# A decode-attention kernel: ScalarE issues the first quarter of the query weights ahead of its small rows, SP the other three quarters

## The chip, the cores and the metric

The kernel runs on one core of a Trainium2 chip. The metric is device time in microseconds (us) for one launch, shown as the median of several runs. The profile names the engines PE (TensorE, matmul), PEld (its weight loads), DVE (VectorE), ACT (ScalarE), POOL (GpSimd) and SP (SyncE, which here only issues transfers). SP's and ACT's queues for DMA instructions are shown as SPq and ACTq; the packets that come from them run under the names q1 (SP) and q10 (ACT) on the same 16 DMA engines.

## What is computed

One token is decoded. Its row `x` (448 values) is normalised. Part A is attention: queries from `xn @ wq` for 16 heads of 256, over a cache of 8 key-value heads with 65536 positions each, then a product with `wo`. Part B is a small gated network on the same row, scaled by a sigmoid of `xn @ w_r`. The output is one row of 448 values.

```
xn = _layernorm(x)
q  = (xn @ wq).reshape(B, Sq, Hq, Dh)            # 448 x 4096 weights
scores = einsum("bhqd,bhkd->bhqk", q, k) * Dh**-0.5
o  = einsum("bhqk,bhkd->bhqd", softmax(scores), v) @ wo
r  = xn @ w_r
y  = (silu(xn @ w_gate) * (xn @ w_up)) @ w_down * sigmoid(r)
out = x + o + xn + y
```

The K and V caches are 256 MiB each in bf16, and every byte of them is read once.

## The kernel before

The caches come in units: one head's keys or values in four units of 8 MiB (128 positions for each of 128 partitions). SBUF holds a ring of three slots of this size. Keys go to slots 0 and 1 in turn, values to slot 2. The first five K units come as two halves (K0 first half, K0 second half, and so on), each with a semaphore of its own, later ones whole. Since all four K units of a head are needed before its softmax, the order is: K0 to K3, V0, K4, K5, then one V and one K unit in turn.

SP issues all the large loads in one list, in that order, and waits in the list: K2's first half needs the first half of slot 0 to be read by PE (`FREEH`), its second half needs all of slot 0 read (`FREE`), K3's halves the same of slot 1; V0 needs the query projection done, whose weights lie in slot 2. Ahead of K0 the list has the query weights `wq` in two parts, one quarter and three quarters of every partition's row, both on one semaphore.

Before PE's main loop there is a chain that makes the queries. ACT issues two small rows, `x` and `w_r` (896 bytes each), on one semaphore (`w0`). DVE first clears some tiles and then waits for both rows. Then come: a cast of x to fp32 (L368), its mean (L370, L372), the subtraction (L375), the sum of squares (L377, L380), a square root on ACT (L405), the scaling and a cast back (L383 to L387), copies that order the row (L393); PE turns it to columns, DVE copies these (L412 to L414), PE multiplies with `wq` (it waits for both parts), DVE scales the result (L416), PE transposes it, DVE copies it to `qT_sb` (L419). POOL fills constants meanwhile and at last clears `kt_all` (L356).

PE then enters its loop over K units. For each set of positions it transposes keys into `ps_t`, DVE (L490) and ACT (L492) copy them to `kt_all`, PE multiplies them with the queries into `ps_q`, ACT copies the scores (L514), PE transposes these into `ps_s`. From unit 4 on, each K unit is joined by one V unit of the head before. PE's last transpose on a slot frees it for SP.

All PE instructions have one line in the profile (L428), and all DMA issues L949, as helpers record them.

Of the kernel before, what the change touches and what calls it, by code (L numbers as in the profile page):

```python
# [22 lines left out]
def bass_parallel_sum__gqa_block_cached__moe_arch_mod__decode_kernel(  # L23
# [54 lines left out]
    WQN, WGN, WDN, WON = RP * HqDh // 2, RP * F, FH * D, rep * NH * D  # L78
# [17 lines left out]
    wq_area = slots[2][:, 0:WQN]  # L96
# [99 lines left out]
    prog = {e: [] for e in engines}  # L196
    here = [("S", 0)]
# [13 lines left out]
    def W(e, *key):  # L211
        put(e, "w", key, None, None)
# [3 lines left out]
    def O(e, key, fn, sem=None, n=1):  # L216
        key = key if isinstance(key, tuple) else (key,)
        if not ghost[0]:
            weight[key] = n
        put(e, "o", key, fn, sem or e)  # L220
# [19 lines left out]
    semtot = {}  # L240
    fed = {}

    def item(key, parts, need=()):
        for n in need:
            W("sp", *n)
        for ap, src, sem in parts:
            semtot[sem] = semtot.get(sem, 0) + 16
            items[key] = (sem, semtot[sem])
            prog["sp"].append(("d", here[0], ("DMA", key, len(prog["sp"])), (ap, src), sem))
# [16 lines left out]
    def flat_src(src, n):  # L266
        return src.rearrange("a b -> (a b)").rearrange("(p n) -> p n", p=P)
# [21 lines left out]
        slot_item("v", t, 2, None, [("VFREE", t - 1)] if t else [("QT",), ("R",), ("CONST",)])  # L289

    WQ1 = WQN // 4
    item("wq", [(wq_area[:, a:b], flat_src(A_wq, WQN)[:, a:b], "wq") for a, b in ((0, WQ1), (WQ1, WQN))])
    for u in range(U):
        k_item(u)
    v_item(0)
# [102 lines left out]

    def act_setup():
        a = nc.scalar  # L400
        for k, (d, s) in enumerate([(x_row, A_x[0]), (wr_row, B_w_r.rearrange("(o n) -> o n", o=1))]):
            prog["act"].append(("d", here[0], ("w0", k), (d, s), "w0"))
        items["w0"] = ("w0", 32)
        W("act", "VPE")
        O("act", "SQRT", lambda it: a.activation(out=stat[0:1, 3:4], in_=stat[0:1, 2:3], func=ACTF.Sqrt), "evq")  # L405
        W("act", "R")
        O("act", "SIG", lambda it: a.activation(out=stat[0:1, 6:7], in_=stat[0:1, 5:6], func=ACTF.Sigmoid), "ev3")
        W("dve", "XNT")
        x = ps_m[0:P, C_XNT:C_XNT + 2 * NE].rearrange("p (t r) -> p r t", t=2)
        xv = xnT_sb.rearrange("p (r b t) -> p r b t", b=2, t=2)  # L410
        y, z = xv[:, :, 0, :], xv[:, 0:NE - 1, 1, :]
        O("dve", "xnt0", lambda it: nc.vector.tensor_copy(out=y, in_=x), "exp")  # L412
        O("dve", "xnt1", lambda it: nc.vector.tensor_copy(out=z[:, :, 0], in_=x[:, 1:NE, 1]))
        O("dve", "XNTSB", lambda it: nc.vector.tensor_copy(out=z[:, :, 1], in_=x[:, 0:NE - 1, 0]))  # L414
        W("dve", "QROW")
        O("dve", "QROWSB", lambda it: nc.vector.tensor_scalar(  # L416
            out=q_row[0:QROWS, :], in0=q_rows[0:QROWS, :], scalar1=inv_sqrt_dh, scalar2=None, op0=ALU.mult))
        W("dve", "QT")
        O("dve", "QTSB", lambda it: nc.vector.tensor_copy(  # L419
            out=qT_sb[:, :, :], in_=ps_m[0:P, C_Q:C_Q + NH * Hq].rearrange("p (q f) -> p f q", f=NH)), "pc", 2)  # L420
        W("act", "QTSB")
        W("act", "S2Z")
# [482 lines left out]
    pool_setup()  # L905
    dve_setup()
    act_setup()
    pe_setup()
    for u in range(NU):
# [275 lines left out]
```

## Time and profile before

| | |
|---|---|
| time, median of 3 runs | 1275.9 us (1275.61 to 1275.92) |
| the profiled execution | 1275.73 us, span 1274.4 us |
| PE busy | 960.9 us, 75% |
| DVE busy | 576.2 us, 45% |
| ACT busy | 436.4 us, 34% |
| POOL busy | 11.6 us, 1% |
| read from HBM | 549.03 MB, 431 GB/s over the span |

Span is from the first to the last recorded instruction of the profiled execution. In a timeline's line stand start, duration, engine, code line, operation and tiles; the brackets at its end give the idle time of the engine ahead of it and what ended that. A DMA issue's last number is the time from issue to landing. In a table of windows each engine has its busy time and count, and the last three columns are PE's granted clock, the busy share of the DMA engines, and GB/s.

### The profile page before, as it was taken

What the parts mean: (1) busy time and instruction counts of PE and PEld (TensorE: products, weight loads), DVE (VectorE), ACT (ScalarE), POOL (GpSimd) and SP (SyncE); (2) the same over time, 40 slices, a digit from 0 to 9 for tenths busy, and PEclk for the clock granted to TensorE, in tenths of its full rate; (3) what the DMA queues carried; (4) which work ended last, traced back from release to release, by engine and by line L of the source; (5) the groups of instructions that cost most, each with busy time, mean ns of one, the idle gap of its engine ahead of it and who ended that gap; (6) DMA issues with size and microseconds to landing.
All of it is one profiled execution on the core that took longest, in us unless ns stands there. A gap on an engine that the chain in (4) does not pass through costs nothing.

```text
span 1274.4 us, 23463 instructions
## 1 busy us (share of the span) xinstructions
PE 960.9 (75%) x9691; PEld 623.0 (49%) x9691; DVE 576.2 (45%) x1083; ACT 436.4 (34%) x656; POOL 11.6 (1%) x38
## 2 busy tenths in 40 slices
PE   3898977778777679777778776787777787777674
PEld 2676654445544455444455444554444554444321
DVE  5666544355344455343454444453444544444310
ACT  1555433244332434233333243343333333323300
POOL 3000000000000000000000000000000000000000
PEclk9999988799888899887898888898888988888875
DMA  9999999999999999999999999999999999999998
GB/s 408 428 435 436 440 428 430 432 432 442 436 428 430 434 432 442 434 430 428 436 432 444 430 430 428 436 432 444 430 430 430 434 438 438 430 430 430 430 431 369
DMA packets 12356, 549.18 MB, mean 431 GB/s; under 512 B 1335, under 2 KB 1722, under 8 KB 2874
## 3 DMA queue, kind: packets, MB, share of 16 engines
q1 hardware_dynamic: 12340, 549.03, 99.8%
q8 instruction: 7, 0.11, 0.0%
q14 instruction: 3, 0.02, 0.0%
q10 hardware_dynamic: 6, 0.00, 0.0%
HBM read 549.03 MB, written 0.00 MB: 431 GB/s over the span
## 4 chain that ended last, share of the span: by engine, by line
DMA 77%; PE 19%; ACT 2%; issue 1%; DVE 1%; SPq 0%; ACTq 0%; DVEq 0%
DMA ring<-in_A_v_cache_dram 68%; PE ps_o L428 13%; DMA ring<-in_A_k_cache_dram 4%; PE ps_t L428 3%; DMA ring<-in_A_wo_dram 2%; DMA kt_all<-in_A_wo_dram 2%; PE ps_q L428 2%; ACT kt_all L492 1%; PE ps_m L428 1%; SPq L949 0%; DVE kt_all L490 0%; PE ps_s L428 0%; ACT S_sb L573 0%; DVE kt_all L731 0%; DVE ring L854 0%
## 5 line engine op out<-in xcount | busy, mean ns | idle before, releaser
L428 PE MATMUL ps_t<-ident_f,ring 128*128 128x128 f32 x4096 | 584.5, 284 | 75.3 <-DMA ring<-in_A_k_cache_dram 48.2
L490 DVE COPY kt_all<-ps_t 128x1024 bf16<-128x1024 bf16 x768 | 486.8, 684 | 281.7 <-PE ps_q L428 277.5
L428 PEld LDWEIGHTS ps_t<-ident_f,ring 128*128 128x128 f32 x4096 | 449.1, 143 | 226.7 <-issue 138.2
L492 ACT ACTIVATE kt_all<-ps_t 128x1024 bf16<-128x1024 bf16 x256 | 261.9, 1023 | 497.1 <-PE ps_q L428 497.0
L428 PE MATMUL ps_o<-ring,p_sb 128*4 128x512 bf16 x2040 | 184.7, 526 | 202.9 <-DMA ring<-in_A_v_cache_dram 198.5
L428 PEld LDWEIGHTS ps_o<-ring,p_sb 128*4 128x4 bf16 x2040 | 54.2, 104 | 295.5 <-issue 271.3
L428 PE MATMUL ps_q<-kt_all,q_cur 128*2 128x512 bf16 x2056 | 163.8, 395 | 0.4 <-DVE kt_all L490 0.3
L514 ACT ACTIVATE s<-ps_q 98x512 bf16<-98x512 f32 x257 | 151.6, 590 | 1.3 <-PE ps_q L428 1.3
L596 DVE RECIPROCAL rs<-ps_m 128x4 f32<-128x4 f32 x29 | 5.3, 183 | 278.5 <-PE ps_m L428 278.5
L583 ACT ACTIVATE p_sb<-S_sb 128x128 bf16<-128x128 bf16 x64 | 18.9, 307 | 269.6 <-PE ps_o L428 267.0
L428 PEld LDWEIGHTS ps_s<-sel_bf,s 128*128 128x128 bf16 x1032 | 64.5, 98 | 5.3 <-ACT s L514 1.9
L428 PE MATMUL ps_s<-sel_bf,s 128*128 128x8 bf16 x1032 | 63.6, 167 | 1.3 <-ACT s L514 1.3
L639 DVE CAST ob_sb<-ps_o 100x512 bf16<-100x512 f32 x29 | 20.1, 692 | 91.4 <-PE ps_o L428 91.4
L428 PEld LDWEIGHTS ps_q<-kt_all,q_cur 128*2 128x2 bf16 x2056 | 26.5, 79 | 43.6 <-issue 43.6
L428 PEld LDWEIGHTS ps_m<-rowsum,ones_f 128*128 128x128 f32 x58 | 12.5, 269 | 23.9 <-issue 23.9
L492 ACT ACT_TABLE_LOAD x7 | 9.0, 1283 | 21.7 <-PE ps_q L428 21.7
L543 DVE TENSOR_REDUCE m1p<-S_sb (+1 forms) x33 | 13.9, 422 | 4.4
L428 PE MATMUL ps_m<-rowsum,ones_f 128*128 128x4 f32 x58 | 15.1, 330 | 0.0
L541 DVE CAST S_sb<-ps_s 128x256 f32 (+1 forms) x33 | 13.7, 414 | 1.9 <-PE ps_s L428 1.9
L573 ACT ACTIVATE S_sb<-S_sb,negmax 128x512 bf16<-128x512 bf16 x16 | 13.2, 852 | 3.2 <-DVE negmax L567 3.2
L428 PE MATMUL ps_m<-diag,ones_f 2*128 2x2 f32 x58 | 11.2, 260 | 3.7 <-DVE diag L558 0.8
L428 PEld LDWEIGHTS ps_m<-diag,ones_f 2*128 2x128 f32 x58 | 8.7, 187 | 10.5 <-DVE diag L558 10.5
(97 smaller groups left out, 136.4 us busy)
## 6 DMA issues: line engine op xcount, KB each, us to landing
ring<-in_A_k_cache_dram SPq DMA_DIRECT2D x10, 4096.0 KB, 28.3
ring<-in_A_v_cache_dram SPq DMA_DIRECT2D x1, 4096.0 KB, 20.6
ring<-in_A_wq_dram SPq DMA_DIRECT2D x1, 2688.0 KB, 11.2
ring<-in_A_wo_dram SPq DMA_DIRECT2D x1, 2688.0 KB, 28.7
ring<-in_A_v_cache_dram SPq DMA_DIRECT2D x1, 2048.0 KB, 24.8
ring<-in_B_w_gate_dram SPq DMA_DIRECT2D x1, 1568.0 KB, 16.4
ring<-in_B_w_up_dram SPq DMA_DIRECT2D x1, 1568.0 KB, 19.8
ring<-in_B_w_down_dram SPq DMA_DIRECT2D x1, 1568.0 KB
```

The source lines that it names most:

```text
L428: return pe.matmul(*a, **k)
L490: O(e, ("EV", s, m), lambda it: nc.vector.tensor_copy(out=kt[:, :], in_=tb[:, :]), f"ev{m}")
L492: O(e, ("EV", s, m), lambda it: nc.scalar.activation(out=kt[:, :], in_=tb[:, :], func=ACTF.Copy), f"ev{m}")
L514: O("act", ("EVQ", s), lambda it: nc.scalar.activation(out=s2[s % 2][0:QROWS, :], in_=ps_q[0:QROWS, :], func=ACTF.Copy), "evq")
L541: O("dve", ("SCOPY", u), lambda it: nc.vector.tensor_copy(out=S_sb[:, at(it, SBN), :], in_=ps_sn), "sc")
L543: O("dve", ("SMAX", u), lambda it: nc.vector.tensor_reduce(out=m1p[:, :, at(it, 1)], in_=S_sb[:, at(it, SBN), :].rearrange("p n i -> p i n ...
L573: O("act", ("EXP", h, i), lambda it, i=i: nc.scalar.activation(out=S_sb[:, :, i], in_=S_sb[:, :, i], func=ACTF.Exp, bias=negmax[:, i:i + 1 ...
L583: O("act", ("PC", t, c), lambda it: nc.scalar.activation(out=p_sb[:, c, :, :], in_=S_sb[:, n:n + CH, :], func=ACTF.Copy), "pc")
L596: O("dve", ("RS", t), lambda it: nc.vector.reciprocal(out=rs[:, :, :], in_=ps_m[0:P, C_TOT:C_TOT + NH * rep]))
L639: O("dve", ("OB", t), lambda it: nc.vector.tensor_copy(out=ob_sb[0:OROWS, :], in_=ps_o[0:OROWS, :]))
```

## The change

The first quarter of the query weights leaves SP's list and becomes the first DMA that ACT issues, ahead of `x` and `w_r`. SP's list now begins with the other three quarters. The semaphore of the weights counts both as before (16 from each).

```
     WQ1 = WQN // 4
-    item("wq", [(wq_area[:, a:b], flat_src(A_wq, WQN)[:, a:b], "wq") for a, b in ((0, WQ1), (WQ1, WQN))])
+    wq_parts = [(wq_area[:, a:b], flat_src(A_wq, WQN)[:, a:b]) for a, b in ((0, WQ1), (WQ1, WQN))]
+    semtot["wq"] = 16
+    item("wq", [(*wq_parts[1], "wq")])
     for u in range(U):
         k_item(u)
...
     def act_setup():
         a = nc.scalar
+        prog["act"].append(("d", here[0], ("wq", 0), wq_parts[0], "wq"))
         for k, (d, s) in enumerate([(x_row, A_x[0]), (wr_row, B_w_r.rearrange("(o n) -> o n", o=1))]):
             prog["act"].append(("d", here[0], ("w0", k), (d, s), "w0"))
         items["w0"] = ("w0", 32)
```

More of the change, by code (lines that the diff above doesn't have):

```diff
@@ L291, in bass_parallel_sum__gqa_block_cached__moe_arch_mod__decode_kernel @@
     WQ1 = WQN // 4
-    item("wq", [(wq_area[:, a:b], flat_src(A_wq, WQN)[:, a:b], "wq") for a, b in ((0, WQ1), (WQ1, WQN))])
+    wq_parts = [(wq_area[:, a:b], flat_src(A_wq, WQN)[:, a:b]) for a, b in ((0, WQ1), (WQ1, WQN))]
+    semtot["wq"] = 16
+    item("wq", [(*wq_parts[1], "wq")])
     for u in range(U):
@@ L400, in act_setup @@
         a = nc.scalar
+        prog["act"].append(("d", here[0], ("wq", 0), wq_parts[0], "wq"))
         for k, (d, s) in enumerate([(x_row, A_x[0]), (wr_row, B_w_r.rearrange("(o n) -> o n", o=1))]):
```

## The prediction

> **What bounds the kernel now.** The page first: the slices, the queues and the chain.
>
> ```profile
> span 1274.4 us, 23463 instructions
> ...
> q1 hardware_dynamic: 12340, 549.03, 99.8%
> HBM read 549.03 MB, written 0.00 MB: 431 GB/s over the span
> DMA 77%; PE 19%; ACT 2%; issue 1%; DVE 1%; SPq 0%; ACTq 0%; DVEq 0%
> ```
>
> SP's queue (q1) keeps the 16 DMA engines busy for 99.8% of the span. At 549.03 MB nothing that an engine computes shows in the time, unless it leaves the DMA engines without work, at the start, at the end, or because SP issues a transfer too late. The change touches the start, so I go to the first microseconds of the DMA view (slices of 0.2 us) and to the timelines of SP and ACT.
>
> ```profile
> GB/s 0 0 0 0 0 0 0 0 143 251 220 143 143 179 358 430 358 466 435 430 358 538 757 645 358 108 466 753 430 108 430 753 430 108 430 753 430 108 430 753
> ...
> 1.00:2.00 1.00, 0.00 (x0) 0.00 (x0) 0.48 (x1) 0.48 (x1) 0.84 (x8) 1.00 0.50 79
> 2.00:3.00 1.00, 0.00 (x0) 0.00 (x0) 0.84 (x3) 0.80 (x1) 1.00 (x9) 1.00 0.68 209
> 3.00:4.00 1.00, 0.00 (x0) 0.00 (x0) 0.85 (x3) 0.00 (x0) 1.00 (x8) 1.00 1.04 424
> ...
> 0.74 0.86 SPq L949 DMA_DIRECT2D ring<-in_A_wq_dram  x2
> ...
> 0.73 0.52 ACTq L949 DMA_DIRECT2D ring<-in_A_x_dram  x1
> 1.28 0.21 ACTq L949 DMA_DIRECT2D ring<-in_B_w_r_dram  x1
> 1.52 1.28 ACT L405 ACT_TABLE_LOAD   x1 [1.52 <-PEq L1170]
> 13.43 0.20 ACT L405 ACTIVATE stat<-stat 1x1 f32<-1x1 f32 x1 [10.62 <-DVE stat L380]
> ```
>
> The first bytes move at 1.6 to 1.8 us, 0.9 to 1.1 after SP's first issue (0.74), and full rate is there by 4. SP and ACT both begin at 0.73 to 0.74, so the first byte cannot come earlier. What a fuller start could give is the shortfall against 431 GB/s between 1.75 and 4: (0.25 x 431 + 431) - (79 + 209) in the first two stretches, some 0.25 MB, or 0.6 us.
>
> **The change, part by part.** *SP loses its first issue* (0.86 / 2 = 0.43 us); everything behind it is issued 0.43 earlier. Worth nothing: the queue is full from 4 us on. In the first two us two queues now feed the engines: between +0.3 and -0.6 us (the shortfall above as the bound of the gain, half of it as that of a loss from switching queues); I take 0, since the bytes and the first issue are as before.
>
> *ACT gains one issue*, ahead of its small rows: 0.43 by SP's row, 0.52 by ACT's own first. Its table load moves from 1.52 to about 2.0, and still ends 10 us ahead of its use at 13.43: nothing. The weights land in sum when they did; their use is covered below.
>
> *The small rows go behind the first quarter.* This is the part that can cost. ACT's queue (q10) shares the 16 engines with q1. Four narrow stretches of the DMA view show how x and w_r get through now; the lines are those of 2.02:2.14, 2.14:4.42, 4.42:4.48 and 4.48:5.0.
>
> ```profile
> DMA packets 6, 0.03 MB, mean 246 GB/s; under 512 B 1, under 2 KB 2, under 8 KB 6
> q10 hardware_dynamic: 2, 0.00, 5.3%
> ...
> q1 hardware_dynamic: 107, 0.77, 88.5%
> q14 instruction: 1, 0.01, 1.5%
> ...
> DMA packets 6, 0.04 MB, mean 612 GB/s; under 512 B 2, under 2 KB 3, under 8 KB 5
> q10 hardware_dynamic: 2, 0.00, 5.2%
> ...
> DMA packets 31, 0.32 MB, mean 607 GB/s; under 512 B 13, under 2 KB 13, under 8 KB 18
> ...
> ring<-in_A_wq_dram SPq DMA_DIRECT2D x1, 2688.0 KB, 11.2
> ring<-in_A_wq_dram SPq DMA_DIRECT2D x1, 896.0 KB, 5.2
> ring<-in_A_k_cache_dram SPq DMA_DIRECT2D x1, 4096.0 KB, 20.4
> ```
>
> x passes at 2.02 to 2.14. w_r, issued 0.55 later, passes only at 4.42 to 4.48, 2.3 us after x. One engine's share of the first quarter is 896 KB / 16 at 431/16 GB/s, 2.13 us: w_r waited for just that share, then went ahead of the second part (rows of 8 KB and more begin in the same stretch), though that part had been issued 0.1 us before it. So I read an engine's turn as one transfer's whole share (8 rows and a semaphore write), with the two queues taking turns: x, first part, w_r, second part. After the change ACT's queue holds first quarter, x, w_r in that order, and SP's the three quarters, the first half of K0, the second half. Turns: quarter (2.13 us), three quarters (6.39), x, half of K0 (4096 KB: 9.73), w_r. From 2.05 that is 2.05 + 18.25 = 20.3; w_r now lands 0.6 before DVE starts (4.45 against 5.04 below), so DVE would start at 20.9 where it starts at 5.04.
>
> The Trainium skill, "DMA: Bandwidth & Descriptors", section "Queues, rings and completion order", says that an engine goes round its queue rows by packets and drains a packet, about 9 to 17 descriptors, before it switches. A share of 8 rows and a semaphore write is nine, so the trace's turn fits it; if instead the packet were filled by count, x and w_r with their two writes would share one turn, w_r would pass before K0, and the sum would be that of the second rival.
>
> *What waits for w_r*: DVE's first cast, and the whole query chain behind it. DVE's timeline:
>
> ```profile
> 5.04 3.75 DVE L368 CAST ring<-ring 1x448 f32<-1x448 bf16 x1 [0.69 <-DMA ring<-in_B_w_r_dram]
> 9.65 2.91 DVE L375 TENSOR_SCALAR ring<-ring,stat 1x448 f32<-1x448 f32 x1
> 13.85 0.44 DVE L385 TENSOR_SCALAR ring<-ring,stat 1x448 f32<-1x448 f32 x1
> 14.32 0.38 DVE L387 CAST ring<-ring 1x448 bf16<-1x448 f32 x1
> 20.61 0.19 DVE L419 CAST qT_sb<-ps_m 128x32 bf16<-128x32 f32 x1 [0.42 <-PE ps_m L428]
> ...
> 8.81 3.51 POOL L356 MEMSET kt_all<- 128x4096 bf16 x1
> ...
> 23.15 0.45 PE L428 MATMUL ps_t<-ident_f,ring 128*128 128x128 f32 x1 [2.65 <-issue]
> ```
>
> The chain takes 20.80 - 5.04 = 15.8 us. Two of its steps run long beside POOL (3.75 and 2.91, where the same work takes 0.38 and 0.44 once POOL is done at 12.3). Late, they cost 3.37 and 2.47 less: 9.9 us. So the chain ends at 20.9 + 9.9 = 30.8 instead of 20.8, and PE, which needs 2.65 us of its own between that chain and its first K transpose, starts at 33.2: 10.0 later. The first quarter of the weights is no issue: both parts land by 1.19 + 11.2 = 12.4.
>
> *Does a late PE matter?* PE frees the ring slots that SP waits for. PE's pace from its start, what it waited for, SP's issues, and issue to landing of the four K halves that need a freed half slot (issued at 35.7, 49.5, 60.9 and 72.3):
>
> ```profile
> 23.12:34.74 11.62, 11.50 (x102) 8.19 (x103) 6.61 (x12) 4.62 (x7) 0.00 (x0) 0.86 1.00 430
> 34.74:72.31 37.57, 33.85 (x348) 25.24 (x347) 24.40 (x41) 19.16 (x27) 0.00 (x0) 1.00 1.01 431
> ...
> SPq L949 <- PE ps_t L428: 89.1, 6, 31.8
> ...
> 35.68 36.96 SPq L949 DMA_DIRECT2D ring<-in_A_k_cache_dram  x4
> ...
> ring<-in_A_k_cache_dram SPq DMA_DIRECT2D x1, 4096.0 KB, 26.0
> ring<-in_A_k_cache_dram SPq DMA_DIRECT2D x1, 4096.0 KB, 21.9
> ring<-in_A_k_cache_dram SPq DMA_DIRECT2D x1, 4096.0 KB, 20.2
> ring<-in_A_k_cache_dram SPq DMA_DIRECT2D x1, 4096.0 KB, 18.5
> ```
>
> PE is busy nearly throughout (one stop of 2.6 us is its own issue), so its delay passes on whole to these issues. A half slot that finds an idle queue would land after 9.73 + 1.0 (to the first packet) + 0.6 (to the waiter) = 11.3 us; by the first quarter's row, 5.2 where its bytes take 2.13, after 9.73 + 3.1 = 12.8. Spare time is therefore 14.7, 10.6, 8.9 and 7.2 us at the four issues by the first price, 1.5 less by the second. A delay of 10.0 passes the first two and not the last two: the DMA engines run dry ahead of the second half of K3, for 10.0 - 7.2 = 2.8 to 10.0 - 5.7 = 4.3 us. I take the middle, 3.5, as the refill has something of a cold start.
>
> Behind it the stream is not cut again. These are V1's landing and what PE waits for before K4:
>
> ```profile
> PE ps_t L428 <- DMA ring<-in_A_k_cache_dram: 2.0, 1, 2.0
> ...
> ring<-in_A_v_cache_dram SPq DMA_DIRECT2D x1, 27.5
> ```
>
> PE has 2.0 us of waiting of its own there, so V1's issue is 8.0 late, against 27.5 - 2 x 9.73 - 1.6 = 6.4 spare plus the 3.5 by which the stream is late itself.
>
> The sum goes against the profiled execution, 1275.73 us (span 1274.4 and 1.3 around it): 1275.73 + 0 + 3.5 = 1279.2. The median, 1275.9, is 0.17 above that run, so 1279.4, which is 0.27% slower. About 0.2% (2.6 us) is what a measurement of this kernel can tell from no change.
>
> **The rivals.**
>
> *Two turns late.* If SP's three quarters get the first turn on the engine that carries the small rows, the order is three quarters, quarter, half of K0, x, other half, w_r: 2.05 + 6.39 + 2.13 + 2 x 9.73 = 30.0, DVE at 30.6, the chain's end at 40.5, PE 19.7 late, a dry spell of 12.5 to 14.0: about 1289. For it: SP and ACT issue within 0.01 us of each other. Against it: x, issued 0.01 ahead of the first part, took the first turn on its engine.
>
> *Early rows, no loss (the other side).* If the engines change queue at every row, the quarter's 8 rows alternate with 8 of the three quarters' (2.13 + 6.39 = 8.5 us), x passes at about 10.6, and w_r with the two semaphore writes after some four K rows of 9.73 / 8 = 1.2: under 15.5, DVE by 16.1. If w_r shares x's turn, DVE starts at 11.3 and the chain ends 0.4 late. The deciding point is the spare 5.7 to 7.2 us: the chain may end as late as 26.5 to 28.0, so DVE may start as late as 16.6 to 18.1. Below that the whole delay is covered and the time is 1275.9, or down to 1275.3 with the fuller start. For it: an instruction packet (q14) got in amid the first part's rows. Against it: w_r's 2.3 us behind exactly one share, and its semaphore write next to it.
>
> The Trainium skill's section "Issuing engines are not separate DMA queues" on the same page says that transfers from different engines interleave and that a second issuer saves only sequencer time; by that alone the sum would be 1275.9, and the row of w_r speaks against so smooth an interleaving.
>
> *The gain that the change could be after*, an earlier stream: bounded at 0.6 us above, 0.05%, so it cannot show as faster.
>
> **How the numbers follow.** One turn late: 0.48, with its own range 1275.9 + 2.8 - 0.6 to 1275.9 + 4.3 + 0.3, 1278.1 to 1280.5; an eighth of it is below the 0.2% line (0.06 same, 0.42 slower). Two turns late: 0.18, all slower. Early rows: 0.34 (0.31 same, 0.02 faster and 0.01 slower for what I have not seen). Together 0.02 faster, 0.37 same, 0.61 slower. The range takes in the likeliest case and the early one, 1275.3 to 1281, and leaves out the 0.18 of two turns.
>
> **What would show it.** DVE's first cast (L368) at about 21 instead of 5.04, at 0.4 us long instead of 3.75; two packets of q10 near 10.6 and two near 20.3; PE's first K transpose near 33; the last K half before V0 issued near 82 and landing 11 to 13 us later instead of 18.5; slices of low GB/s between 70 and 85 us. The forecast is wrong if the cast starts before 16, if PE makes up time between its start and 72 us, or if the cast starts near 31.

## The result and the profile after

The changed kernel takes 1278.47 us (median of 20 runs, 1276.73 to 1280.99) against 1275.72 (20 runs, 1275.54 to 1275.92): a ratio of 1.0023, 95% interval 1.0017 to 1.0030. It is 2.75 us slower, and its runs spread over 4.3 us where those of before spread over 0.4. The profiled execution is one of its shorter ones: 1277.34 us, span 1276.0.

The page of the changed kernel, queues and chain:

```profile
span 1276.0 us, 23463 instructions
q1 hardware_dynamic: 12196, 548.12, 99.5%
q10 hardware_dynamic: 150, 0.92, 0.2%
HBM read 549.03 MB, written 0.00 MB: 430 GB/s over the span
DMA 75%; PE 19%; ACT 3%; issue 1%; DVE 1%; SPq 0%; ACTq 0%; DVEq 0%
```

The kernel is the same stream of transfers as before, with the quarter of the weights now under ACT's queue (q10). To see where the stream lost time, take the start first: the timelines of ACT, DVE and PE. (The helpers' lines, and those of the chain, are numbered two or three higher than before: a DMA issue is L952, PE L431, DVE's first cast L370.)

```profile
0.73 0.42 ACTq L952 DMA_DIRECT2D ring<-in_A_wq_dram  x1
1.18 0.54 ACTq L952 DMA_DIRECT2D ring<-in_A_x_dram  x1
1.75 0.24 ACTq L952 DMA_DIRECT2D ring<-in_B_w_r_dram  x1
...
16.31 0.38 DVE L370 CAST ring<-ring 1x448 f32<-1x448 bf16 x1 [11.95 <-DMA ring<-in_B_w_r_dram]
25.95 0.19 DVE L422 CAST qT_sb<-ps_m 128x32 bf16<-128x32 f32 x1 [0.42 <-PE ps_m L431]
...
28.49 1.94 PE L431 MATMUL ps_t<-ident_f,ring 128*128 128x128 f32 x8 [2.64 <-issue]
```

DVE waits for w_r until 16.31 instead of 5.04, its chain then takes 9.83 us, and PE's first K transpose comes at 28.49 instead of 23.15. How the small rows were held up shows in narrow stretches of the DMA view: 4 to 10 us, and two of 0.06 us at 12.2 and 14.66.

```profile
q1 hardware_dynamic: 83, 1.78, 69.7%
q10 hardware_dynamic: 93, 0.67, 26.4%
...
DMA packets 2, 0.03 MB, mean 561 GB/s; under 512 B 0, under 2 KB 1, under 8 KB 1
...
DMA packets 4, 0.10 MB, mean 1653 GB/s; under 512 B 0, under 2 KB 1, under 8 KB 1
```

In those 6 us the engines took 83 rows of SP's queue and 93 of ACT's, that is, one of each in turn. The lone packets under 2 KB are x and w_r; a K row of 32 KB (1.2 us) begins beside them. Between x and w_r (12.26 to 14.66) and behind w_r (14.72 to 16) ACT's queue has one packet each, the only one under 512 B, a semaphore write of 4 bytes:

```profile
DMA packets 32, 1.02 MB, mean 423 GB/s; under 512 B 1, under 2 KB 1, under 8 KB 1
...
DMA packets 22, 0.69 MB, mean 538 GB/s; under 512 B 1, under 2 KB 1, under 8 KB 1
```

They pass at 13.45 and 15.91. So behind the quarter's rows came its semaphore write, x, x's write, w_r and w_r's write, 1.2 us apart, which is one K row between each and the next.

Now the place where the delay meets the stream. SP's issue of the second half of K3 in the changed kernel, and the landing times of the four K halves that wait for a freed half slot, in order:

```profile
77.20 0.33 SPq L952 DMA_DIRECT2D ring<-in_A_k_cache_dram  x1
...
ring<-in_A_k_cache_dram SPq DMA_DIRECT2D x1, 4096.0 KB, 20.8
ring<-in_A_k_cache_dram SPq DMA_DIRECT2D x1, 4096.0 KB, 17.1
ring<-in_A_k_cache_dram SPq DMA_DIRECT2D x1, 4096.0 KB, 15.4
ring<-in_A_k_cache_dram SPq DMA_DIRECT2D x1, 4096.0 KB, 14.8
```

The last is issued 4.9 us late (77.20 against 72.31) and takes 14.8 to land instead of 18.5, so it lands at 92.0 instead of 90.8: 1.2 us lost there. The windows of 3 us around it, first of before and then of the changed kernel (last column GB/s), show the gap:

```profile
76.00:79.00 3.00, 2.91 (x32) 2.19 (x30) 2.05 (x5) 1.51 (x2) 0.00 (x0) 1.00 1.04 448
79.00:82.00 3.00, 2.91 (x31) 2.07 (x29) 2.71 (x6) 1.51 (x2) 0.00 (x0) 1.00 0.99 426
82.00:85.00 3.00, 2.82 (x34) 2.08 (x36) 1.89 (x3) 1.51 (x2) 0.00 (x0) 1.00 1.04 448
```

```profile
76.00:79.00 3.00, 2.82 (x33) 2.06 (x29) 1.89 (x3) 1.51 (x2) 0.00 (x0) 1.00 0.87 371
79.00:82.00 3.00, 2.91 (x34) 2.19 (x31) 1.89 (x3) 1.61 (x4) 0.00 (x0) 1.00 1.03 360
82.00:85.00 3.00, 2.91 (x31) 2.19 (x31) 2.83 (x7) 1.67 (x3) 0.00 (x0) 1.00 0.94 393
```

In these 9 us the changed kernel moves (448 + 426 + 448 - 371 - 360 - 393) x 3 = 0.6 MB less, 1.4 us of the full rate. Of the 1.6 us that this execution is longer, 0.4 or so does not show in that landing.

### The profile page after: what moved, and what is told of

Same layout as the page of the kernel before. It is cut to its first block, busy times and chain, and to the rows that moved or that the text cites. A ratio compares the mean times of both kernels' runs of the same rounds, so it can differ in the third digit from the quotient of the medians.

```text
span 1276.0 us, 23463 instructions
## 1 busy us (share of the span) xinstructions
PE 951.6 (75%) x9691; PEld 619.7 (49%) x9691; DVE 570.0 (45%) x1083; ACT 436.4 (34%) x656; POOL 8.0 (1%) x38
## 4 chain that ended last, share of the span: by engine, by line
DMA 75%; PE 19%; ACT 3%; issue 1%; DVE 1%; SPq 0%; ACTq 0%; DVEq 0%
DMA ring<-in_A_v_cache_dram 71%; PE ps_o L431 13%; PE ps_t L431 4%; ACT kt_all L495 3%; DMA kt_all<-in_A_wo_dram 2%; PE ps_q L431 2%; DMA ring<-in_B_w_r_dram 1%; PE ps_m L431 1%; SPq L952 0%; DVE kt_all L493 0%; ACT S_sb L576 0%; PE ps_s L431 0%; ACTq L952 0%; DVE ring L419 0%; ACTq L1057 0%
## 5 line engine op out<-in xcount | busy, mean ns | idle before, releaser
L431 PE MATMUL ps_t<-ident_f,ring 128*128 128x128 f32 x4096 | 583.3, 284 | 76.5 <-DMA ring<-in_A_k_cache_dram 49.9
L431 PEld LDWEIGHTS ps_t<-ident_f,ring 128*128 128x128 f32 x4096 | 447.6, 143 | 228.0 <-issue 137.9
L431 PE MATMUL ps_o<-ring,p_sb 128*4 128x512 bf16 x2040 | 180.0, 515 | 207.7 <-DMA ring<-in_A_v_cache_dram 203.3
L431 PEld LDWEIGHTS ps_o<-ring,p_sb 128*4 128x4 bf16 x2040 | 53.8, 103 | 298.0 <-issue 272.1
L431 PE MATMUL ps_q<-kt_all,q_cur 128*2 128x512 bf16 x2056 | 163.6, 395 | 0.3 <-DVE kt_all L493 0.3
L431 PEld LDWEIGHTS ps_s<-sel_bf,s 128*128 128x128 bf16 x1032 | 64.0, 97 | 5.0 <-ACT s L517 1.9
L431 PE MATMUL ps_s<-sel_bf,s 128*128 128x8 bf16 x1032 | 63.3, 167 | 1.3 <-ACT s L517 1.3
L431 PEld LDWEIGHTS ps_q<-kt_all,q_cur 128*2 128x2 bf16 x2056 | 26.3, 79 | 44.5 <-issue 44.5
L431 PEld LDWEIGHTS ps_m<-rowsum,ones_f 128*128 128x128 f32 x58 | 12.3, 264 | 22.0 <-issue 22.0
L431 PE MATMUL ps_m<-sel_bf,ring 1*128 1x1 bf16 (+1 forms) x12 | 0.6, 167 | 21.6 <-DVE ring L395 20.8
L431 PE MATMUL ps_m<-rowsum,ones_f 128*128 128x4 f32 x58 | 14.8, 326 | 0.0
L431 PE MATMUL ps_m<-diag,ones_f 2*128 2x2 f32 x58 | 11.2, 260 | 3.6 <-DVE diag L561 0.6
## 6 DMA issues: line engine op xcount, KB each, us to landing
ring<-in_B_w_gate_dram SPq DMA_DIRECT2D x1, 1568.0 KB, 16.1
```

Of the source, the lines that this page charges most:

```text
L431: return pe.matmul(*a, **k)
```

## The experiments

Theory 1: the change costs because w_r is late; that delays DVE, then PE, then SP's issue of K3's second half, and only what goes past the spare time there is lost. Theory 2: two queues at the start cost by themselves.

**The small rows first, the quarter behind them.** Two queues as in the change, but x and w_r early.

```
     def act_setup():
-        prog["act"].append(("d", here[0], ("wq", 0), wq_parts[0], "wq"))
         for k, (d, s) in enumerate([(x_row, A_x[0]), (wr_row, ...)]):
             prog["act"].append(("d", here[0], ("w0", k), (d, s), "w0"))
         items["w0"] = ("w0", 32)
+        prog["act"].append(("d", here[0], ("wq", 0), wq_parts[0], "wq"))
```

> ACT issues x, w_r and then the quarter; SP still begins with the three quarters, so two queues feed the engines as in the change. Theory 1 (the lateness of w_r alone costs: it delays DVE, so PE, so SP's issue of K3's second half): w_r passes within about 3 us of its issue, DVE's first cast starts at 4 to 6, PE's first K transpose at 23 to 24, time 1275.4 to 1276.0 with a spread below 0.5. Theory 2 (two queues at the start cost by themselves, through switching or engines left uneven): PE at 23 to 24 too, but time 1277 to 1279.5.

Measured: 1275.94 us (11 runs, 1275.72 to 1276.07) against 1275.77, ratio 1.0000, interval 0.9991 to 1.0009. First PE's entry into the second half of its loop body in the kernel before; then, here, DVE's cast, the same entry of PE, and SP's issue of K3's second half with its landing:

```profile
38.31 1.07 PE L428 MATMUL ps_t<-ident_f,ring 128*128 128x128 f32 x8 [2.57 <-issue]
...
6.92 2.04 DVE L370 CAST ring<-ring 1x448 f32<-1x448 bf16 x1 [2.56 <-DMA ring<-in_B_w_r_dram]
...
40.53 1.44 PE L431 MATMUL ps_t<-ident_f,ring 128*128 128x128 f32 x8 [3.32 <-issue]
...
75.85 0.33 SPq L952 DMA_DIRECT2D ring<-in_A_k_cache_dram  x1
...
ring<-in_A_k_cache_dram SPq DMA_DIRECT2D x1, 4096.0 KB, 15.3
```

Theory 2 falls. The cast came at 6.92, later than expected, and PE at 24.49. PE's lateness is not the cast's here: the quarter, issued at 1.53 behind the small rows, took 16.1 us to land, and PE stopped for 4.2 us ahead of its product with `wq`, until 17.67. The last two rows were not foreseen: PE started 1.3 late, yet the issue at K3 is 3.5 late, and that cost nothing. PE's stop ahead of the second half of its loop body (shown as "issue": the profile shows nothing that it waited for) was 3.3 us here against 2.57 before, and it ran slower after it, at a granted clock of 0.50 between 42.4 and 44.3.

**One queue, the rows later still.** The kernel before, with x and w_r issued by SP between the halves of K0.

```
     for u in range(U):
         k_item(u)
+        if u == 0:
+            half = prog["sp"].pop()
+            item("w0", [(x_row, A_x[0], "w0"), (wr_row, ..., "w0")])
+            prog["sp"].append(half)
...
-        for k, (d, s) in enumerate([(x_row, A_x[0]), (wr_row, ...)]):
-            prog["act"].append(("d", here[0], ("w0", k), (d, s), "w0"))
```

> One queue only: the kernel before, but SP issues x and w_r between the two halves of K0 and ACT issues nothing. They pass behind the first half of K0, at 20.5 to 20.7. Theory 1: DVE's first cast at about 21.3, PE's first K transpose at about 33.3, 10.1 late; against the change (5.3 late, 2.7 us lost) the loss grows by the added 4.8, to 1281 to 1284. Theory 2: no second queue, 1275.4 to 1276.0.

Measured: 1283.07 us (5 runs, 1282.05 to 1284.12), ratio 1.0058, interval 1.0044 to 1.0072.

```profile
21.36 0.38 DVE L372 CAST ring<-ring 1x448 f32<-1x448 bf16 x1 [17.00 <-DMA ring<-in_B_w_r_dram]
...
83.03 0.33 SPq L950 DMA_DIRECT2D ring<-in_A_k_cache_dram  x1
...
ring<-in_A_k_cache_dram SPq DMA_DIRECT2D x1, 4096.0 KB, 12.0
```

Lateness alone, without a second queue, costs 7.3 us in the median. In the profiled execution the issue of K3's second half is 10.7 us later than before, and the time 6.3 us longer. That is theory 1.

**V0 ahead of K3's second half.** The changed kernel, with more transfers in the queue where it ran dry.

```
     for u in range(U):
         k_item(u)
+    n_v0 = len(prog["sp"])
     v_item(0)
+    v0 = prog["sp"][n_v0:]
+    del prog["sp"][n_v0:]
+    prog["sp"][n_v0 - 2:n_v0 - 2] = v0
     k_item(U)
```

> The changed kernel with one move: SP issues V0 ahead of K3's second half, so 19.5 us of transfers lie in the queue when that half becomes free to issue. Theory 1: DVE's first cast still at about 16.3 and PE's first K transpose at about 28.5, but no engine runs dry between 70 and 85 us; time 1275.4 to 1276.2, spread below 0.6. Theory 2: the start is the same as in the change, so the time stays at 1277.5 to 1279.5.

Measured: 1276.26 us (11 runs, 1275.97 to 1277.80), ratio 1.0006, interval 0.9997 to 1.0015. PE was as late as in the change (28.72), so the loss does sit at that issue: of 2.75 us some 0.5 is left, with three of 11 runs above 1277. K3's first half is now the tight one in the profiled execution:

```profile
ring<-in_A_k_cache_dram SPq DMA_DIRECT2D x1, 4096.0 KB, 14.6
```

**V0 ahead of both halves of K3** (in the same edit, `n_v0 - 4` for `n_v0 - 2`).

> The changed kernel, with V0 issued ahead of both halves of K3 instead of ahead of the second. With V0 ahead of the second half alone, a few runs were still 1 to 2 us long, which would be the queue running low at K3's first half. Theory 1: PE starts as late as in the change (28.3 to 28.9), K3's first half lands 30 us or more after its issue, the time is 1275.5 to 1276.2 in all runs. If what is left comes from elsewhere (the start itself), the median stays at 1276.3 and some runs at 1277 and above.

Measured: 1276.12 us (11 runs, 1275.80 to 1279.47), ratio 1.0008, interval 0.9999 to 1.0017. The median lies where it was expected, though 0.14 below the run with V0 ahead of one half is no clear difference; the long runs do not go: three of 11 are at 1277.6 to 1279.5. K5 and V1, the next that wait for PE, land in the profiled execution (1275.88 us) after

```profile
ring<-in_A_k_cache_dram SPq DMA_DIRECT2D x1, 24.9
ring<-in_A_v_cache_dram SPq DMA_DIRECT2D x1, 24.8
```

where they took 31.0 and 27.5 before. A whole unit has 9.73 us more to move than a half. By the 14.0 to 14.8 us that a half took on a queue that was just running low (table below), a unit there needs, by this estimate, 23.7 to 24.5: 0.3 to 1.2 us to spare. That the long runs are cut there would fit, but none of them was profiled, so it stays open.

**Only w_r behind the quarter.** ACT issues x, quarter, w_r.

```
         for k, (d, s) in enumerate([(x_row, A_x[0]), (wr_row, ...)]):
             prog["act"].append(("d", here[0], ("w0", k), (d, s), "w0"))
+            if k == 0:
+                prog["act"].append(("d", here[0], ("wq", 0), wq_parts[0], "wq"))
```

> ACT issues x, then the quarter, then w_r: one semaphore write less and one small row less stand ahead of w_r, each of which cost one row of K0 (1.2 us) in the changed kernel. Theory 1 (rows in turn, and the delay counts only past the spare time at K3's second half): w_r passes at about 12.2, DVE's first cast starts at 13.6 to 14.2, PE's first K transpose at 25.7 to 26.5, some 2.9 late instead of 5.3. If the spare time is the 3 to 4 us that the first runs suggest, the time is 1275.6 to 1276.5; if it were below 1 us, 1277.5 or more. Theory 2 (two queues cost by themselves): as the change, 1277.5 to 1279.5.

Measured: 1279.39 us (8 runs, 1278.36 to 1280.70), ratio 1.0027, interval 1.0016 to 1.0037: worse than the change, not better. w_r passed at 15.9 to 16.1 and DVE's cast began at 17.65. The quarter, issued 0.55 us later than in the change, found SP's rows lined up ahead of it. The stretches 2:5.7 and 5.7:6.1 of the DMA view:

```profile
q1 hardware_dynamic: 54, 1.16, 82.2%
...
q1 hardware_dynamic: 7, 0.15, 87.4%
q10 hardware_dynamic: 14, 0.10, 59.5%
```

54 rows of SP's went first; only then did the turns begin, and the quarter's last rows stood among K0's. My expectation had missed this head start. Counted from the start, these are the rows of SP's queue that passed ahead of the quarter's first, in the changed kernel (to 3.16) and here (to 5.75):

```profile
q1 hardware_dynamic: 16, 0.34, 45.5%
...
q1 hardware_dynamic: 63, 1.35, 68.1%
```

That is one row for each of the 16 engines where SP and ACT issued together, and four where ACT's quarter came 0.55 us later. It bears on the lateness, not on theory 1, which it supports: later cast, longer time.

**The changed kernel again, three times**, unedited, for its spread.

> The changed kernel once more, to see why its runs spread over 4 us. Theory A: PE's way from its start to K2's second half varies (its stop in front of the loop's second half took 2.2 to 3.3 us in the runs so far), and each us of it goes into SP's issue of K3's second half: a run that is longer by n us has that issue later by about n, at 76.5 to 81. Theory B: the place of w_r among the K rows varies: DVE's first cast then starts at other times than 16.3, in steps of 1.2. Theory C: both are as before (cast 16.3, issue 77.2) and only the refill of the dry engines varies.

> The changed kernel a third time, for the same comparison: time against the start of DVE's first cast (16.3 in the first profile) and the issue of K3's second half (77.2). Theories A, B and C as for the second.

> The changed kernel once more, as a test of the line found so far: the issue of K3's second half at 76.5 gave 1275.8, at 77.2 gave 1277.3 and at 80.0 gave 1280.4. Here the issue time should tell the time within 0.7 us: 1275.8 up to 76.5, and beyond it about 1275.8 + 1.3 x (issue - 76.5).

Measured: 1275.80, 1280.35 and 1276.96 us. DVE's cast began at 16.54, 16.71 and 16.30: theory B falls. The issue at K3 was at 76.55, 79.97 and 77.08, not the same: theory C falls as the main cause. The third is 0.4 us above what its issue time should give. PE's entry into the second half of the loop body and SP's issue at K3 in the second of them:

```profile
44.70 1.94 PE L431 MATMUL ps_t<-ident_f,ring 128*128 128x128 f32 x8 [2.41 <-issue]
...
79.97 0.33 SPq L952 DMA_DIRECT2D ring<-in_A_k_cache_dram  x1
```

and in the first, where PE did not stop there for its own issue at all:

```profile
42.55 1.07 PE L431 MATMUL ps_t<-ident_f,ring 128*128 128x128 f32 x8 [0.18 <-ACT kt_all L495]
...
76.55 0.33 SPq L952 DMA_DIRECT2D ring<-in_A_k_cache_dram  x1
```

PE's way between the two issues for K2 was 11.4, 14.9 and 13.4 us in the three, and from PE's start to the second of them 24.9, 28.2 and 25.9. That is theory A: in one and the same kernel this way varies by 3.3 us. The stop is one part of it (0.2, 2.4 and 2.2 us). The pace after the stop is another: in the second of them the eight transposes there took 1.94 us, in the third 1.07. The 2 us from that entry on, in the second and in the third (PEclk is the third number from the end):

```profile
44.70:46.70 2.00, 2.00 (x12) 1.64 (x16) 0.00 (x0) 0.00 (x0) 0.00 (x0) 0.50 1.06 459
```

```profile
43.09:45.09 2.00, 2.00 (x20) 1.38 (x21) 0.26 (x1) 0.27 (x1) 0.00 (x0) 1.00 0.84 360
```

PE was granted half its clock there in the one and all of it in the other, behind stops of 2.41 and 2.18 us. What makes the stop vary is not shown. All profiled executions with V0 in its old place, but for the two below with the weights cut by partitions, by the issue of K3's second half:

| kernel | issue | issue to landing | time of that execution |
|---|---|---|---|
| before | 72.31 | 18.5 | 1275.73 |
| small rows first | 75.85 | 15.3 | 1275.94 |
| change, second | 76.55 | 14.4 | 1275.80 |
| change, fourth | 77.08 | 14.0 | 1276.96 |
| x on its own semaphore (below) | 77.16 | 14.1 | 1276.35 |
| change, first | 77.20 | 14.8 | 1277.34 |
| only w_r late | 79.68 | 14.5 | 1280.61 |
| change, third | 79.97 | 14.5 | 1280.35 |
| rows late, one queue | 83.03 | 12.0 | 1282.05 |

Up to 76.5 nothing is lost: the spare time is 4.2 us. Past it the time goes up by about the delay, with 1.1 and 1.7 us more in the two at 80. In these two, K2's second half (14.6 and 14.7 us to land) and K3's first (14.4 and 15.3) already took hardly longer than K3's second, and with the rows late 12.2 both: a larger delay empties the queue from K2's second half on. The loss does not add up over the three: in the change's third execution K3's second half lands 3.7 us later than before, and 7.7 us late less 4.2 is 3.5.

**x on a semaphore of its own.** The change's transfers; DVE's first cast waits for x alone, w_r is awaited ahead of its product.

```
-            prog["act"].append(("d", here[0], ("w0", k), (d, s), "w0"))
-        items["w0"] = ("w0", 32)
+            prog["act"].append(("d", here[0], ("w%d" % k, 0), (d, s), "w%d" % k))
+            items["w%d" % k] = ("w%d" % k, 16)
...
+        W("dve", "DMA", "w1")
         O("dve", "R", ...)
```

> The changed kernel with one thing undone on the waiting side: x and w_r have a semaphore each, DVE's first cast waits for x alone, and w_r is awaited only ahead of its product (L398), 4.4 us later in the chain. Transfers and their order are the change's. Theory 1: the cast starts at 13.6 to 14.2 (x passes at 12.2 to 12.4, its semaphore write one K row later), PE's first K transpose at 25.8 to 26.5, SP's issue of K3's second half at 73 to 77, landing 14.4 to 18; with spare time to an issue of about 76.4 most runs are at 1275.6 to 1276.2. If the two queues or the refill cost by themselves: 1277.5 to 1279.5 as in the change.

Measured: 1276.09 us (11 runs, 1275.78 to 1279.41), ratio 1.0005, interval 0.9995 to 1.0014. The cast began at 13.84 and PE at 26.11. With 2.4 us of lateness taken off and every transfer as in the change, some 2.4 of its 2.75 us are gone; two runs are still above 1277, which PE's stop can do. The profiled execution does not show the gain at K3: PE needed 15.1 us between the two issues for K2 (a stop of 2.57, then a granted clock of 0.50), so the issue came at 77.16, as late as in the change. The case for this edit is its median.

**The quarter cut by partitions**: ACT takes 32 whole rows, SP the other 96.

```
-    wq_parts = [(wq_area[:, a:b], flat_src(A_wq, WQN)[:, a:b]) for a, b in ((0, WQ1), (WQ1, WQN))]
+    wq_parts = [(wq_area[a:b, :], flat_src(A_wq, WQN)[a:b, :]) for a, b in ((0, P // 4), (P // 4, P))]
```

> ACT's quarter is 32 whole partition rows (2 of 28 KB for each engine) instead of a quarter of all 128 rows (8 of 7 KB for each engine); bytes, order and issuers as in the change. If the engines take rows of the two queues in turn, x passes after 4 rows of 28 KB (4.3 us) at about 6.3 and w_r after three more rows at about 9.5, DVE's first cast starts at 10 to 10.5 and PE's first K transpose is at 22.5 to 24. Theory 1: time 1275.4 to 1276.0. Theory 2: 1277 to 1279.5.

Measured: 1283.80 us (5 runs, 1283.53 to 1284.03). DVE's cast began at 19.07, not at 10 to 10.5. It says nothing on the two theories, as the weights themselves came at half the rate: by 20 us 4.66 MB had moved, before 7.84, and that is 7.4 of the 8.0 us. To see whether that takes two queues, the same cut with SP issuing both parts and ACT only the small rows (in the kernel before):

> To find why the cut by partitions cost 8 us (28 KB rows took 1.9 to 2.2 us where 21 KB rows take 0.8): the kernel before, with SP issuing 32 partition rows and then the other 96, one queue. If the cut alone slows the engines, the weights land some 6 us later and the time is 1281 to 1284; if it takes two queues that read both parts at once, the time is 1275.6 to 1276.3.

Measured: 1284.00 us (4 runs, 1283.84 to 1284.28). The stretch 6 to 10 us with the cut by partitions in two queues, then in one; before, this stretch had 430:

```profile
6.00:10.00 4.00, 0.00 (x0) 0.00 (x0) 0.00 (x0) 0.00 (x0) 2.75 (x1) 1.00 1.07 244
```

```profile
6.00:10.00 4.00, 0.00 (x0) 0.00 (x0) 2.54 (x4) 0.00 (x0) 2.72 (x1) 1.00 0.97 215
```

The DMA engines are as busy (1.07 and 0.97) and move half. The cut does it, with either number of queues.

No version beat the kernel before: where PE's delay is hidden, the time is that of the stream.

## Why the prediction came out as it did

The time (1279.4 forecast, 1278.47 measured) and the chain of causes were right; two of its terms were off by much, in opposite directions, and that they nearly cancelled was luck.

- *What bounds it, and the start.* Right. Two queues at the start cost nothing that shows (small rows first: 1.0000).
- *The turn of an engine.* Wrong. I read w_r's 2.3 us wait in the trace of before as one transfer's whole share and forecast the cast at 20.9. The engines take row by row (83 to 93 packets in 6 us), and the cast came at 16.31, as my second rival had worked out (by 16.1), just above the 16 below which I had called the forecast wrong. The sign that I gave, packets of ACT's queue near 10.6 and 20.3, did not come: x passed at 12.2, w_r at 14.7. What I took for a turn was, by the head start of SP's rows in "only w_r late", rather rows lined up before w_r was there: 54 rows of 21.5 KB there, eight of 7 KB for that engine before. How long the head start is I cannot say: it was one row for each engine in the change and four in "only w_r late".
- *The rule of the Trainium skill that I set beside it* ("DMA: Bandwidth & Descriptors", "Queues, rings and completion order": an engine drains a packet of some 9 to 17 descriptors before it switches). The trace of the changed kernel does not agree: one row each in turn, and single semaphore writes between K rows.
- *DVE's chain of 9.9 us and PE's 2.65.* Right: 9.83 and 2.64. (2.65 is PE's stop, which begins ahead of DVE's last copy; from the end of that copy to the first K transpose it is 2.35 us before and after, and the sum went by that.)
- *PE's delay passes on whole.* Right in the mean of four executions of the changed kernel (PE 5.5 late, the issue 5.4), but I took its stop of 2.6 us, and its pace after it, for fixed. The stop was nil to 3.3, the granted clock behind it 0.50 or 1.00, and with the spare time used up each us of it shows: that is most of the spread of 4.3 us.
- *The spare time at K3's second half.* Mis-sized: 5.7 to 7.2 forecast, 4.2 measured. I priced a landing behind an idle queue at 11.3 to 12.8 us. It was 12.0 where the queue was idle (rows late), but 14.0 to 14.8 in all executions where it had only just run low. The difference lies between the engines. A landing is that of the last of 16 semaphore writes; these are the stretches in which the 16 of K3's second half pass, before (88.2 to 90.5) and with the rows late (94.1 to 94.8):

```profile
DMA packets 37, 1.21 MB, mean 527 GB/s; under 512 B 16, under 2 KB 16, under 8 KB 16
...
DMA packets 32, 1.05 MB, mean 1498 GB/s; under 512 B 16, under 2 KB 16, under 8 KB 16
```

  Before, the 16 are spread over 2.1 us; behind an idle queue, from which all engines start together, over 0.6. At the issue of 76.55 they are still spread over 2.0: a queue that has only just run low still has work for its last engine, and I take it that the landing waits for that one.
- *The second rival's "no loss"* fell by this term: it put the deciding point at a cast of 16.6 to 18.1. With 4.2 us to spare, against a PE that was 5.3 late at 16.31, it lies near 15.2, and the cast at 16.31 was past it.
- *No second cut behind it.* Right for the change: V1 landed 27.1 us after an issue at 142.33, 1.1 us later than before, as K3 had. What the delayed executions lose beyond K3's landing (0.4 us in the first, up to 2.1 with the rows late) is in part this same spread. With the rows late, the 16 writes are 5.4 us later in the mean, where the last is 4.3 later. In the first, the last 16 writes of `wo`, at the end, are 1.1 us later in the mean, and the last of them 1.6. The rest I cannot place.

So the likeliest case had the right size for partly wrong reasons: half the delay (5.3 for 10.0), against two thirds of the spare time (4.2 for 5.7 to 7.2). Either error alone would have missed: 5.3 us against 5.7 to 7.2 gives no loss, 10.0 against 4.2 gives 5.8.

## What to carry to other kernels

A transfer put ahead of a small one on the same queue delays it by the other queue's rows as well, since the DMA engines serve both in turn; a small row that starts a serial chain goes first, and gets a semaphore of its own. In a kernel bound by its stream, find the issue with the shortest time from issue to landing: what it has above the floor (here 18.5 against 14.4) is all that the engines may lose ahead of it. A delay that uses up such a margin showed here as spread too, because stops and a lower clock that were hidden before now count.

## What the runs showed of the hardware that was not expected

- The two queues are served one row, one semaphore write at a time: 83 against 93 packets in 6 us, and four K rows of 1.2 us between the quarter's semaphore write and w_r's.
- Loads cut into 32 and 96 partitions ran at 215 to 244 GB/s where 128 partitions ran at 430, with the engines fully busy. Why was not tried.
- SP's rows that passed ahead of the first row of ACT's quarter were 16 where both were issued together and 63 where the quarter was issued 0.55 us later.
- PE's stop ahead of the second half of its loop body took from none to 3.3 us in executions of nearly the same program (2.2, none, 2.4 and 2.2 in four of the changed kernel). The granted clock behind it was 0.50 in some (stops of 2.41 and 2.57) and 1.00 in others (2.18, 2.19 and, before, 2.57), so the length of the stop alone does not decide it.
- The 16 engines finish a transfer up to 2.1 us apart while the queue never empties, and 0.6 apart behind an idle queue.
